# A fused mLSTM cell and SwiGLU block: the value halves of four weight pieces are asked for by GpSimd instead of ScalarE and SP

## The chip, the cores and the metric

The kernel runs on one core of one Trainium2 chip. The time is that of the device for one execution, in microseconds (us); three runs of the kernel before gave 554.77, 555.38 and 555.61, median 555.38. A profile shows one further execution.

The core has five engines, each with its own instruction stream in fixed order: TensorE (PE; its weight loads are listed as PEld), VectorE (DVE), ScalarE (ACT), GpSimd (POOL) and SyncE (SP, which here only asks for DMA transfers). ScalarE and GpSimd can ask for transfers too. All transfers run on 16 shared DMA engines; each asking engine has a queue of its own there. Engines and transfers wait for each other by semaphores.

## The reference

Two blocks follow each other. The first is an mLSTM cell over 4 batches, 8 heads, 768 steps and head size 40; the second a SwiGLU feed-forward layer on its output, 3072 tokens of 320 features, with 1536 hidden units.

```python
for t in range(S):                                   # per batch and head
    m_new = max(f[t] + m, i[t])
    C = exp(f[t] + m - m_new) * C + exp(i[t] - m_new) * outer(v[t], k[t])
    n = exp(f[t] + m - m_new) * n + exp(i[t] - m_new) * k[t]
    y[t] = sigmoid(o[t]) * (C @ q[t]) / max(abs(n @ q[t]), 1)
x = y, as (tokens, heads * head size)                # 3072 x 320
g = x @ w_gate;  val = x @ w_val                     # 320 x 1536 each
out = (g * sigmoid(g) * val) @ w_out                 # 1536 x 320
```

The three weights arrive as 64-bit floats; everything else is fp32.

## The kernel before, in words

**Stages.** The 768 steps are cut into six groups of 128 tokens for each of the 4 batches, so a group is 512 tokens wide for the feed-forward layer. For group g the kernel runs the 12 blocks of hidden units (`hidden(g, m)`, L643: 10 pairs of matmuls into two PSUM banks, one for gate and one for value, then SiLU on ScalarE, L653, and the product on VectorE, L654), with the mLSTM work of group g+1 set between the blocks by hand (`slots`, L727), and then the projection with `w_out` (L664, L671). The order of instructions on each engine is the order in which the program's text calls them.

**Start.** The first group's mLSTM part has functions of its own (`first_...`, L478 to L562). The calls from L564 to L611 are in the order that each engine follows. Among them are `sig(0)` and `sig(1)` (L463: sigmoid of o_sb on ScalarE, after its load), `first_gate(P)` (L541: two products on VectorE, then a small copy of x_sb on GpSimd, L545), `first_seam` (L555: transposes on PE and copies to xT by ScalarE and VectorE) and `first_state` (L547). `burn` (L466) keeps PE busy with matmuls whose result is not used.

**Weights.** A 64-bit weight is read as two 32-bit words and made into a 32-bit float on the chip. `PIECES` (L138) lists ten pieces: pieces 0 and 1 have one block of 128 hidden units each, pieces 2 to 6 two blocks each, always gate and value; pieces 7 to 9 are w_out. `piece_load(p)` (L140) asks for a piece. The gate half goes to partitions 0 to 63, the value half to partitions 64 to 127; a half of a two-block piece is 640 KB, 64 x 5 rows of 2 KB. The gate half is asked for by SP, the value half by ScalarE for pieces below 5 and by SP from 5 on (L146, L165). Pieces 0, 1, 4 and 5 land in the two buffers `raw` of a pool, piece 2 in a part of h_sb that is not in use yet and piece 3 in wo_sb.

A block j is then converted in three steps: `scale(j)` on ScalarE (L190 the high words, L192 the low words), `join(j)` on VectorE (L199, L200) and `rounded(j)` (L207) on GpSimd, except for block 0 and three later ones, where VectorE does it. Blocks 0 and 1 are converted before the first `hidden`; block m+2 is converted while `hidden(0, m)` runs for the first four (`ahead`, L725). ScalarE's part of block 2 stands in its stream before the SiLU of `hidden(0, 0)`.

**What stands around the change.** ScalarE asks for the value halves of pieces 2 and 3 right behind `sig(1)`, and for that of piece 4 behind `scale(0)`, before its copies for `first_seam(1)`. SP asks for the value half of piece 5 behind that piece's gate half; after it come the store of M_sb to M_dram (L611) and the loads of k and q for the second group (L117). GpSimd has, in this stretch, the two copies of `first_gate` and then `rounded(1)`, `rounded(2)` and so on; it asks for no transfer in the whole kernel.

Of the kernel before, what the change touches and what calls it, by code (L numbers as in the profile page):

```python
# [12 lines left out]
U32 = mybir.dt.uint32  # L13
# [11 lines left out]
def kernel(  # L25
# [18 lines left out]
    nc = tc.nc  # L44
# [12 lines left out]
    NKC = DM // HP  # L57
    UH = BH // 2
    UA = UH // 2
    NH = NFC + 1  # L60
# [15 lines left out]
    def bank(name, tag="cell"):  # L76
        return psum.tile([128, 512], F32, name=name, tag=tag)
# [23 lines left out]
    wo_sb = const.tile([128, NFC, DM], F32)  # L101
    h_sb = const.tile([128, NH, TW], F32)
# [34 lines left out]
    raws = {}  # L137
    PIECES = [("gv", 0, 1), ("gv", 1, 1)] + [("gv", m, 2) for m in range(2, NFC, 2)] + [("o", m, 4) for m in range(0, NFC, 4)]  # L138

    def piece_load(p, home=None):  # L140
        kind, m, n = PIECES[p]
        if kind == "gv":
            a, d = NKC, n * 128
            src = [(slice(i * HP, (i + 1) * HP), w[:, m * 128:(m + n) * 128].rearrange("(c p) f -> p c f", p=HP))
                   for i, w in enumerate((moe_w_gate, moe_w_val))]
            queues = (nc.sync, nc.scalar if p < 5 else nc.sync)  # L146
        else:
            a, d = n, DM
            src = [(slice(0, 128), moe_w_out[m * 128:(m + n) * 128].rearrange("(a p) d -> p a d", p=128))]
            queues = (nc.sync,)  # L150
        if src[0][1].dtype == F32:
            for r, w in src:
                if kind == "o":
                    nc.sync.dma_start(out=wo_sb[r, m:m + n, :], in_=w)
                else:
                    for x in range(n):
                        nc.sync.dma_start(out=wgv_sb[r, m + x], in_=w[:, :, ts(x, 128)])
            return
        if home is None:
            raw = conv.tile([128, 4 * NKC * 128], U32, name="raw")  # L160
        else:
            raw = home.rearrange("p a t -> p (a t)").bitcast(U32)
        raw = raw[:, 0:2 * a * d]
        for (r, w), queue in zip(src, queues):
            queue.dma_start(out=raw[r].rearrange("p (a d) -> p a d", a=a), in_=w.bitcast(U32))  # L165
        words = raw.rearrange("p (a d two) -> p a d two", two=2, a=a)
        raws[p] = (words[:, :, :, 0], words[:, :, :, 1])
        split(p)
# [4 lines left out]
    def split(p):  # L173
        if p in raws:
            lo, hi = raws.pop(p)
            kind, m, n = PIECES[p]
            if kind == "gv":
                for c in range(n):
                    r = slice(c * 128, (c + 1) * 128)
                    blocks[m + c] = (lo[:, :, r], hi[:, :, r], wgv_sb[:, m + c])  # L180
            else:
                for c in range(0, n, 2):
                    blocks[NFC + (m + c) // 2] = (lo[:, c:c + 2], hi[:, c:c + 2], wo_sb[:, m + c:m + c + 2, :])

    def scale(j):
        if j in blocks:
            lo, hi, dst = blocks[j]
            a, d = hi.shape[1], hi.shape[2]
            top = conv.tile([128, NKC * 128], F32, name="top", bufs=1).rearrange("p (a d) -> p a d", a=a)
            nc.scalar.mul(top, hi.bitcast(F32), 2.0 ** -112)  # L190
            low = conv.tile([128, NKC * 128], I32, name="low").rearrange("p (a d) -> p a d", a=a)
            nc.scalar.mul(low, lo, 2.0 ** -29)  # L192
            blocks[j] = (low, top.bitcast(U32), dst)
# [53 lines left out]
    for u in range(B):  # L247
        r = slice(u * BH, (u + 1) * BH)
# [213 lines left out]
    def sig(P):  # L462
        nc.scalar.activation(o_sb[:, heads(P)], o_sb[:, heads(P)], AF.Sigmoid)  # L463


    def burn(n, tag="cell"):  # L466
        t = bank("burn", tag)
        for _ in range(n):
            nc.tensor.matmul(t, lhsT=junk[:, 0:128], rhs=junk, start=True, stop=True)
# [57 lines left out]
    def first_own(u):  # L527
        first_y[u] = bank("first_y", "gen")[:, 0:H * D1].rearrange("p (h d) -> p h d", d=D1)
        for h in range(H):
            nc.tensor.matmul(first_y[u][:, h, :], lhsT=W0[:, u * H + h, :], rhs=v_sb[:, u * H + h, :], start=True, stop=True)  # L530

    def first_x(u):
        y = first_y.pop(u)
        den = work.tile([128, UH, 1], F32, name="den")[:, 0:H]
        nc.vector.tensor_scalar(den, y[:, :, D:], scalar1=1.0, scalar2=None, op0=ALU.max)
        nc.vector.scalar_tensor_tensor(den, in0=y[:, :, D:], scalar=-1.0, in1=den, op0=ALU.mult, op1=ALU.max)
        nc.vector.reciprocal(den, den)
        nc.vector.tensor_tensor(x_sb[:, u, 0:DM].rearrange("p (h d) -> p h d", d=D), y[:, :, 0:D],
                                den.to_broadcast([128, H, D]), op=ALU.mult)

    def first_gate(P):  # L541
        for u in (2 * P, 2 * P + 1):
            x = x_sb[:, u, 0:DM].rearrange("p (h d) -> p h d", d=D)
            nc.vector.tensor_tensor(x, x, o_sb[:, u * H:(u + 1) * H], op=ALU.mult)
        nc.gpsimd.tensor_copy(x_sb[:, 2 * P:2 * P + 2, DM:], x_sb[:, 2 * P:2 * P + 2, 0:HP])  # L545
# [33 lines left out]
    first_turn(1, q_sb, qT, (A, V))  # L579
    load(o_sb, o_gate, 0, 1)  # L580
    piece_load(0)
    piece_load(1)
    late_maxima()
    first_own(1)
# [2 lines left out]
    first_x(1)  # L587
    sig(0)
    sig(1)
    piece_load(2, h_sb[:, NH - NKC:])  # L590
    piece_load(3, wo_sb)
    burn(3)
    first_own(2)
    first_own(3)
    first_gate(0)
    first_x(2)
    first_x(3)
    first_seam(0, (A, A, V))
    scale(0)
    first_gate(1)  # L600
    burn(6, "gen")
    piece_load(4)
    join(0)
# [242 lines left out]
```

## Time and profile before

| | us |
|---|---|
| median of three runs | 555.38 |
| the profiled execution | 555.16 |
| its span, first to last instruction | 553.0 |
| PE busy (99% of the span) | 546.4 |
| VectorE busy (42%) | 234.4 |
| ScalarE busy (24%) | 134.7 |
| GpSimd busy (19%) | 106.6 |

The granted TensorE clock is at full speed throughout. 45.69 MB move in 223,994 packets; the DMA engines are busy nine tenths of the time in the first 83 us and less later. SP's queue (q1) carries 42.11 MB, ScalarE's (q10) 2.85 MB.

In a row of the timeline stand the start and the duration in us, the engine, the line of the program, the operation, output<-input with its size, and how often; in brackets how long the engine stood idle before it and what ended that. SPq, ACTq and POOLq are the instruction sequencers, where requests for transfers appear: their duration is that of asking, not of the transfer. The chain that ended last is followed back from the last instruction, at each step to what released it. Busy matmuls are modelled at their ends, so neighbouring rows overlap by some hundredths.

### The profile page before, as it was taken

The page shows a single profiled execution, that of the slowest core. Times are in us where ns is not written, and L with a number is a line of the kernel's source. Part 1 is how long each engine was busy: PE and PEld are TensorE (multiplying, and loading weights), DVE is VectorE, ACT ScalarE, POOL GpSimd, SP SyncE. Part 2 cuts the span into 40 slices and gives each one's busy share as a digit, 9 for nine tenths or more (in the row PEclk, how much of TensorE's full clock was granted, in tenths as well). Part 3 has the DMA queues.
Part 4 walks back from the last instruction along what each step waited for, and adds up shares of the span by engine and source line. Part 5 has one row for each costly group of instructions (what it writes and reads, how often), then busy time and mean ns, then how long its engine had stood idle before and what let it go on. Part 6 is the DMA issues. An engine that isn't in the chain of part 4 may idle for free.

```text
span 553.0 us, 11595 instructions
## 1 busy us (share of the span) xinstructions
PE 546.4 (99%) x4992; PEld 312.9 (57%) x4992; DVE 234.4 (42%) x394; ACT 134.7 (24%) x202; POOL 106.6 (19%) x97
## 2 busy tenths in 40 slices
PE   8999999999999999999999999999999999999997
PEld 4955546675545575544576455466455567444475
DVE  5956687962156332445521445531426621011100
ACT  4366564443101033110124101005110100111100
POOL 2314355574011151011133001114001200000000
PEclk9999999999999999999999999999999999999999
DMA  9999996798631763660464451395000131000000
GB/s 125 177 280 187 192 274 115 155 111 125 68 49 17 108 109 83 71 76 5 82 127 104 53 68 27 49 149 107 13 1 2 29 62 43 12 1 0 2 24 24
DMA packets 223994, 45.69 MB, mean 83 GB/s; under 512 B 214504, under 2 KB 219112, under 8 KB 223944
## 3 DMA queue, kind: packets, MB, share of 16 engines
q1 hardware_dynamic: 222036, 42.11, 46.7%
q10 hardware_dynamic: 1908, 2.85, 2.0%
q8 instruction: 39, 0.64, 0.5%
q14 instruction: 11, 0.09, 0.1%
HBM read 35.68 MB, written 4.01 MB: 72 GB/s over the span
## 4 chain that ended last, share of the span: by engine, by line
PE 92%; DMA 4%; SPq 3%; POOL 0%; DVE 0%; ACT 0%; issue 0%; ACTq 0%; POOLq 0%
PE gv_ps L648 55%; PE o_ps L664 24%; PE o_ps L671 5%; SPq L117 3%; DMA h_sb<-in_moe_w_val_dram 2%; PE inter L377 2%; PE sp L331 2%; PE intra L382 2%; DMA o_sb<-in_o_gate_dram 2%; PE add L353 1%; PE tp_kq L296 0%; POOL wgv_sb L207 0%; PE tp_x L439 0%; DVE wgv_sb L200 0%; ACT top L190 0%
## 5 line engine op out<-in xcount | busy, mean ns | idle before, releaser
L648 PE MATMUL gv_ps<-xT,wgv_sb 64*128 64x512 f32 x1440 | 317.3, 593 | 1.6 <-POOL wgv_sb L207 1.1
L648 PEld LDWEIGHTS gv_ps<-xT,wgv_sb 64*128 64x128 f32 x1440 | 139.1, 187 | 159.4 <-issue 154.6
L654 DVE TENSOR_TENSOR h_sb<-sg,gv_ps 128x512 f32<-128x512 f32 x72 | 49.5, 687 | 214.5 <-ACT sg L653 214.4
L664 PE MATMUL o_ps<-wo_sb,h_sb 128*128 128x320 f32 x480 | 130.5, 433 | 0.0
L664 PEld LDWEIGHTS o_ps<-wo_sb,h_sb 128*128 128x128 f32 x480 | 90.8, 190 | 41.0 <-issue 3.8
L653 ACT ACTIVATE sg<-gv_ps 128x512 f32<-128x512 f32 x72 | 43.0, 597 | 268.6 <-PE gv_ps L648 268.5
L362 POOL TENSOR_TENSOR C<-C,dec 128x328 f32<-128x328 f32 x20 | 14.5, 735 | 137.7 <-DVE C L369 137.6
L456 POOL TENSOR_SCALAR_AFFINE_SELECT w_sb<-w_sb 64x1024 f32<-64x1024 f32 x20 | 27.8, 1388 | 60.2 <-DVE w_sb L451 59.3
L658 ACT COPY z_sb<-o_ps 128x320 f32<-128x320 f32 x24 | 10.0, 422 | 94.7 <-PE o_ps L664 90.9
L403 POOL TENSOR_TENSOR o_sb<-o_sb,y_sb 128x640 f32<-128x640 f32 x10 | 14.3, 1428 | 79.2 <-DVE y_sb L394 79.1
L671 PE MATMUL o_ps<-wo_sb,h_sb 128*128 128x320 f32 x96 | 26.9, 437 | 0.0
L451 DVE TENSOR_TENSOR w_sb<-g_T,w_sb 128x1024 f32<-128x1024 f32 x10 | 13.2, 1355 | 27.6 <-DMA w_sb<-M_dram 27.6
L426 DVE STREAM_TRANSPOSE xT<-x_sq 128x640 f32<-128x640 f32 x16 | 12.5, 822 | 23.7 <-DMA x_sq<-x_sb 23.7
L671 PEld LDWEIGHTS o_ps<-wo_sb,h_sb 128*128 128x128 f32 x96 | 17.9, 190 | 7.2
L394 DVE TENSOR_TENSOR y_sb<-y_sb,intra 64x328 f32<-64x328 f32 x40 | 19.7, 493 | 0.8 <-PE intra L382 0.2
L369 DVE TENSOR_TENSOR C<-C,add 40x328 f32<-40x328 f32 (+1 forms) x36 | 17.7, 493 | 1.3 <-PE add L353 0.4
L207 POOL TENSOR_TENSOR wgv_sb<-wgv_sb,low 128x640 int32<-128x640 int32 x8 | 12.3, 1541 | 23.7 <-DVE wgv_sb L200 21.9
L377 PEld LDWEIGHTS inter<-C,qT 64*64 64x64 f32 x640 | 10.2, 134 | 7.3 <-issue 6.1
L341 POOL TENSOR_TENSOR vw_sb<-v_sb,w_sb 128x656 f32<-128x656 f32 x10 | 12.8, 1303 | 0.4
L338 DVE TENSOR_TENSOR w_sb<-sp,w_sb 128x512 f32<-128x512 f32 x20 | 12.7, 682 | 0.0
L460 ACT ACTIVATE w_sb<-w_sb 128x1024 f32<-128x1024 f32 x10 | 10.6, 1058 | 8.8 <-POOL w_sb L456 8.8
L397 DVE TENSOR_SCALAR den<-den 128x16 f32<-128x16 f32 x10 | 12.2, 1216 | 0.3
(129 smaller groups left out, 343.7 us busy)
## 6 DMA issues: line engine op xcount, KB each, us to landing
w_sb<-M_dram SPq DMA_DIRECT2D x10, 512.0 KB, 7.2
x_sq<-x_sb SPq DMA_DIRECT2D x128, 40.0 KB, 2.0
k_sb<-in_k_dram SPq DMA_DIRECT2D x12, 320.0 KB, 6.1
v_sb<-in_v_dram SPq DMA_DIRECT2D x12, 320.0 KB, 5.7
o_sb<-in_o_gate_dram SPq DMA_DIRECT2D x12, 320.0 KB, 5.4
raw<-in_moe_w_out_dram SPq DMA_DIRECT2D x3, 1280.0 KB, 7.8
out_dram<-z_sb SPq DMA_DIRECT2D x24, 160.0 KB, 1.8
q_sb<-in_q_dram SPq DMA_DIRECT2D x32, 64.0 KB, 2.4
```

The lines of the kernel that those rows point to most:

```text
L117: nc.sync.dma_start(out=dst[:, heads(P), 0:D], in_=tokens(a, c, P))
L362: nc.gpsimd.tensor_tensor(state(s + 1)[:, a], state(s)[:, a], dec[:, s - 2, a].unsqueeze(2).to_broadcast([128, UA, D1]), op=ALU.mult)
L369: nc.vector.tensor_tensor(c, c, ps[r], op=ALU.add)
L377: nc.tensor.matmul(inter[two][half(i), a, :], lhsT=qT[half(two), P * UA + a, half(i)], rhs=state(2 * n + i)[half(two), P * UA + a, :], sta ...
L394: nc.vector.tensor_tensor(t, t, intra[i][half(c)], op=ALU.add)
L403: eng.tensor_tensor(o, o, y[:, :, 0:D], op=ALU.mult)
L456: nc.gpsimd.affine_select(w, w, compare_op=ALU.is_ge, fill=NEG, base=0, pattern=[[0, UH], [1, SUB]], channel_multiplier=-1)
L648: nc.tensor.matmul(ps[i], lhsT=wgv_sb[half(i), m, PAIRS[kc][i] if g < 2 else kc, :], rhs=x[half(i), kc, :], start=(kc == 0), stop=(kc == N ...
L653: nc.scalar.activation(sg, ps[0], AF.Silu)
L654: nc.vector.tensor_tensor(hid(g, m), sg, ps[1], op=ALU.mult)
L664: nc.tensor.matmul(p, lhsT=hid(g, m)[:, ts(u, L)], rhs=wo_sb[:, m, :], start=(m == 0), stop=(m == NFC - 1))
L671: nc.tensor.matmul(ps[u], lhsT=hid(g, m)[:, ts(u, L)], rhs=wo_sb[:, m, :], start=(m == 0), stop=(m == NFC - 1))
```

## The change

Three things are different. The value halves of pieces 2 to 5 are asked for by GpSimd. For pieces 2 and 3 the two halves are asked for at different places in the text: the gate half where it was, the value half later, behind `first_gate(0)` and `first_gate(1)`, which end with a copy on GpSimd. And for this the requests of a piece are kept in a small list until they are made (`asks`, `value_half`). Pieces 4 and 5 are called where they were, so on GpSimd the request for piece 4 comes before `rounded(1)` and that for piece 5 between `rounded(1)` and `rounded(2)`. Sizes, buffers and the conversion are as before.

```diff
+    asks = {}
+
+    def value_half(p):
+        for ask in asks.pop(p, ()):
+            ask()
+
-    def piece_load(p, home=None):
+    def piece_load(p, home=None, later=False):
...
-            queues = (nc.sync, nc.scalar if p < 5 else nc.sync)
+            queues = (nc.sync, nc.scalar if p < 2 else nc.gpsimd if p < 6 else nc.sync)
...
-        for (r, w), queue in zip(src, queues):
-            queue.dma_start(out=raw[r].rearrange("p (a d) -> p a d", a=a), in_=w.bitcast(U32))
+        asks[p] = [lambda r=r, w=w, queue=queue: queue.dma_start(out=raw[r].rearrange("p (a d) -> p a d", a=a), in_=w.bitcast(U32))
+                   for (r, w), queue in zip(src, queues)]
+        asks[p].pop(0)()
+        if not later:
+            value_half(p)
...
-    piece_load(2, h_sb[:, NH - NKC:])
-    piece_load(3, wo_sb)
+    piece_load(2, h_sb[:, NH - NKC:], later=True)
+    piece_load(3, wo_sb, later=True)
     burn(3)
     first_own(2)
     first_own(3)
     first_gate(0)
+    value_half(2)
     first_x(2)
     first_x(3)
     first_seam(0, (A, A, V))
     scale(0)
     first_gate(1)
+    value_half(3)
     burn(6, "gen")
     piece_load(4)
```

## The prediction

> **What bounds the kernel now.** I read the page first. TensorE (PE) is busy for 99% of the span, and the chain that ended last is 92% PE; but two of its shares are not PE: 3% is SP's queue and 2% a value half on its way. Read in order of time, that chain shows where (columns: start us, duration us, what):
>
> ```profile
> 16.64 8.77 DMA o_sb<-in_o_gate_dram
> ...
> 25.42 0.01 ACT o_sb L463
> 25.43 13.59 DMA h_sb<-in_moe_w_val_dram
> ...
> 39.17 0.81 ACT top L190
> ...
> 40.01 0.51 DVE wgv_sb L199
> ...
> 40.54 0.84 DVE wgv_sb L200
> ...
> 41.51 1.54 POOL wgv_sb L207
> ...
> 43.10 4.80 PE gv_ps L648 x20
> ```
>
> The value half of piece 2 (the third) is asked for at 25.43, behind ScalarE's wait for o_sb, and lands at 39.02. Then ScalarE, VectorE and GpSimd convert block 2 in 4.08 us (39.02 to 43.10), and hidden(0, 2) starts. From 43.10 to the end the chain is PE, but for 0.33 us at 100.65 and the last copy. So a shift of hidden(0, 2) goes to the end one for one, as long as nothing behind it becomes late. How long PE stood is in its timeline:
>
> ```profile
> 31.90 4.56 PE L648 MATMUL gv_ps<-xT,wgv_sb 64*128 64x512 f32 x20 [0.53 <-DVE m_in L285]
> 36.39 1.13 PE L552 MATMUL add<-vw_sb,k_sb 128*64 128x41 f32 x32
> 37.45 4.56 PE L648 MATMUL gv_ps<-xT,wgv_sb 64*128 64x512 f32 x20
> 43.10 4.80 PE L648 MATMUL gv_ps<-xT,wgv_sb 64*128 64x512 f32 x20 [1.08 <-POOL wgv_sb L207]
> 47.83 0.49 PE L622 MATMUL tp_g<-ident,i_sb 32*128 32x32 f32 x5
> ...
> 53.52 8.85 PE L648 MATMUL gv_ps<-xT,wgv_sb 64*128 64x512 f32 x40
> ```
>
> PE has one hole, 1.08 us. Two blocks that follow each other without a hole take 8.85 us (last row; what follows them starts at 62.38, 8.86 after 53.52), so without it the transposes of L622 could start at 37.45 + 8.86 = 46.31 and not at 47.83: **1.52 us** is all that there is to win here (1.08 idle, 0.24 because the stalled block takes 4.80 and not 4.56, the rest overlap at the seam).
>
> Why 13.6 us for 640 KB? The queue totals of two windows, 26 to 32 us and 33 to 44 us (queue: packets, MB, share of 16 engines):
>
> ```profile
> q1 hardware_dynamic: 809, 1.17, 109.4%
> ...
> q10 hardware_dynamic: 953, 1.87, 53.4%
> q1 hardware_dynamic: 921, 1.79, 50.9%
> ```
>
> q1 is SP's queue, q10 ScalarE's (its 2.85 MB over the span are ScalarE's loads). From 26 to 32 us q10 moves nothing, though its request was out at 25.43 to 26.03; q1 alone brings 196 GB/s. From 33 us both run, 333 GB/s together, and q1 hardly suffers (0.195 MB/us before, 0.163 beside). In the window of 32 to 33 us q10 has its first 28 packets. So the value half stood some 6.5 us behind the gate halves of pieces 2 and 3, asked for by SP at 22.94 and 23.69, and then took 6.6 us (32.4 to 39.02).
>
> **What the Trainium skill says.** "Perfetto Trace Analysis", section "DMA Instruction — HWDGE (DVE, Sync)": the hardware descriptor generator is one block shared by two sequencers and locked until a DMA's descriptors are made. The silent q10 agrees. "DMA: Bandwidth & Descriptors", section "SWDGE vs HWDGE vs iDMA": a DMA of GpSimd has its descriptors made by software on GpSimd and put into rings of its own, and each DMA engine goes round robin over its queues; section "Latency and other measured facts": first byte after about 1 us, against 0.6. No DMA of GpSimd is in this trace. "SBUF — State Buffer", section "SBUF: two separate sides": a two-port VectorE operation and GpSimd lock each other out; a GpSimd DMA of 620 ns alone took 3100 ns beside a copy. The lock is visible here: L199 takes 0.49 us, but 0.89 at 49.39, beside GpSimd's L207 (48.37 to 49.92).
>
> **The change, part by part.**
>
> *Piece 2's value half.* It leaves ScalarE at 25.43 and stands on GpSimd behind first_gate(0)'s copy (25.88 + 0.29 = 26.17), 0.74 us later. Its cost on GpSimd, G, is not in the trace. Bounds: 0.6 (the hardware queues' issue rows, 0.59 to 0.63) and 3.1 (the skill's locked-out case); I take 1.3, near the unlocked end, as VectorE's operations between 26 and 28.6 are mostly PSUM readers or tiny. First packets at 26.17 + 1.3 = 27.5. With the 6.6 us that the same transfer took once it had begun, it lands at 34.1. ScalarE is free for scale(2) only at 35.52 (end of L609, 34.78 + 0.74), so scale(2) starts at 35.6, block 2 is ready 4.0 us later at 39.6, and PE wants it at 42.0. The hole is gone: **−1.52**.
>
> *What GpSimd must also do.* Queued behind the requests are the copy for first_gate(1) (29.09, VectorE releases it), rounded(1) (34.31) and rounded(2). From 26.17 until PE wants block 2 (41.85, one block pitch after 37.45) there are 15.68 us; the copy and two roundings take 0.29 + 1.53 + 1.53 = 3.35; so four requests may take 12.3, G ≤ 3.08 each. With 1.3: request 2 ends 27.5, copy 29.38, requests 3 and 4 end 32.0, rounded(1) runs at 34.31 as before, request 5 35.84 to 37.1, rounded(2) ends before 40. Cost nothing, hidden by GpSimd's idle time (2.92, 4.93 and 5.66 us before those three operations). A VectorE L199 locked out by a request (the ones at 32.8 and 36.5 could be) loses at most G; blocks 1 and 2 have 1.6 (35.84 to 37.45) and 2.3 us to spare.
>
> *Sharing with the gate halves.* hidden(0, 0) hangs without slack on piece 0's gate half: landed 28.42 (the row of L190 at 28.50 waited 0.39 for it), L190, L199, L200, L123, L207 on VectorE until 31.76, PE 31.90. If the new ring starts at 27.5, the last packets of that half meet competition; 0 to 0.5 us, I take **+0.1**, as it is nearly done. Piece 1's half (1.6 us spare) and piece 2's gate half (33.4, at 0.163 instead of 0.195 MB/us about 35) stay in front of their users: ScalarE takes piece 2 at 35.6.
>
> *ScalarE loses three issues* of about 0.6 us. Two stood in front of a wait for PE. The third (30.04 to 30.65) held two copies of xT until 30.69; they end 0.6 earlier, but VectorE's rounding of block 0 ends at 31.76 too, and PE starts after both: 0. Without that cover it would be worth up to 0.6.
>
> *SP loses one issue* and its 3.6 us wait (37.72), so M_dram and the loads of k and q for the next stage move some 4 us ahead. Their users come at 62 us and later: 0. Pieces 3 to 5 are asked for at 29.4, 30.7 and 35.8 (before: 26.07, 30.04, 37.72). On a ring of 0.17 MB/us they end near 36, 40 and 44; ScalarE takes them at about 43, 52 and 56 (before: 45.05, 53.65 and 58.61): 0.
>
> **Sum.** 555.16 (the profiled execution, span 553.0 plus 2.2 around it) − 1.52 + 0.1 = 553.74. The median, 555.38, lies 0.22 higher: **554.0 us**, −0.25%. Anything within 0.2% (1.1 us) is about what a measurement of this kernel can't tell from no change.
>
> **Rivals.**
>
> *The data comes no earlier (0.15).* If requests are served in the order asked whatever the ring, GpSimd's at 27 stands behind SP's at 23.69 as ScalarE's at 25.43 did, starts at 32.4, lands at 39.0: 555.4. For: q10's silence alone doesn't say whether generator or engines held it. Against: from 33 us on the engines take from both queues at once.
>
> *The hole is replaced (0.07).* A late gate half of piece 0 (0.5 us) or of piece 2, or wider tails, leave a gain of 0.2 to 1.0: 554.4 to 555.2. Against: both queues together move 333 GB/s, so the gate loses little.
>
> *GpSimd becomes the bound (0.20), the slower side.* Each request carries 320 rows of 2 KB. Past G = 3.08 GpSimd's own row of work from 26.17 to rounded(2) sets hidden(0, 2), late by 4G − 12.3. The gain is eaten at G = 3.5, and 0.2% is lost at 3.75. With G = 4: 555.38 − 1.52 + 3.7 = 557.6. For: the skill's locked-out 3.1 us, VectorE busy nine tenths of the time in 26 to 34 us, no DMA of GpSimd here to price. Against: most of those VectorE operations are not two-port ones (L199, 0.49 us, is), and the lock ends with each.
>
> **Numbers.** The forecast has 0.58, its own range 553.5 to 554.7 (landing of piece 0's half ±0.4, repeats ±0.3); below 554.27 lie 0.50 of it. The rest of it, the two rivals without gain and a little of the third give 0.30 within 0.2%; slower 0.20. The range 553.4 to 557.0 leaves out the larger values of G and little else.
>
> **What would show it.** Right: a new software queue with packets from about 27.5 us while q1 runs; scale(2)'s L190 at about 35.6 instead of 39.17, with no wait for the value half; no hole before the third block of L648, L622 at 46.3 to 46.4; L123's two ScalarE copies at 30.1; SP's M_dram near 34. Wrong: GpSimd's copy for first_gate(1) later than 29.1 or rounded(1) later than 34.4 (G too large), hidden(0, 0) later than 32.0 (piece 0's gate half), or the new queue silent until 32 us.

## The result, and the profile after

The changed kernel takes 556.44 us (median of 16 executions, 555.56 to 559.57); the kernel before, on the same chip in turn with it, 554.78 us (16 executions, 554.16 to 558.07). The ratio is 1.0029, 95% interval 1.0018 to 1.0039: **slower by 0.3%**, where 0.25% faster was forecast. The profiled execution of the changed kernel took 555.86 us with a span of 554.1, the one of the kernel before 555.16 with 553.0. The changed kernel's own lines move: L648 is L659 now, L622 is L633, L451 is L460, L207 is L216, L190 is L199.

The chain that ended last, of the changed kernel (start us, duration us, what):

```profile
25.95 0.23 POOL x_sb L554
26.18 12.52 DMA h_sb<-in_moe_w_val_dram
...
38.86 0.80 ACT top L199
...
41.20 1.53 POOL wgv_sb L216
...
42.77 4.80 PE gv_ps L659 x20
```

The value half of piece 2 is asked for by GpSimd right behind first_gate(0)'s copy, as forecast, and lands at 38.70 instead of 39.02. The other three steps of its conversion follow as before. So the hole of PE stays, a little smaller. In the timeline of the changed kernel:

```profile
42.77 4.80 PE L659 MATMUL gv_ps<-xT,wgv_sb 64*128 64x512 f32 x20 [0.72 <-POOL wgv_sb L216]
47.51 0.49 PE L633 MATMUL tp_g<-ident,i_sb 32*128 32x32 f32 x5
```

The transposes start at 47.51 and not at 46.3; 0.32 us is won of 1.52. Why the data came no earlier is in the queue totals of the same two windows as before the change, 26 to 32 us (first line) and 33 to 44 us (the others; queue: packets, MB, share of 16 engines):

```profile
q1 hardware_dynamic: 792, 1.18, 109.1%
...
q0 software_dynamic: 540, 2.02, 64.7%
q1 hardware_dynamic: 553, 1.07, 38.5%
```

GpSimd's queue, q0, moves nothing until its first packet at 33.30, 6.3 us after its request was out (26.18 + 0.84 = 27.02), just as ScalarE's q10 did. Then it takes more than its share: 2.02 MB in 11 us, against q1's 1.07. Before, q1 had 1.79 beside ScalarE's 1.87. The sum fell from 3.66 MB to 3.09.

What pays for that is what stands on SP's queue behind the gate halves. Of the timeline of the kernel before, SP's requests, VectorE's first use of w_sb and a stop of PE in `intra`:

```profile
39.01 11.05 SPq L117 DMA_DIRECT2D k_sb<-in_k_dram  x2
...
56.61 9.13 SPq L447 DMA_DIRECT2D w_sb<-M_dram  x2
...
70.97 1.22 DVE L451 TENSOR_TENSOR w_sb<-g_T,w_sb 128x1024 f32<-128x1024 f32 x1 [1.31 <-DMA w_sb<-M_dram]
...
100.98 0.67 PE L382 MATMUL intra<-v_sb,w_sb 64*64 64x41 f32 x30 [0.33 <-issue]
```

And of the changed kernel:

```profile
34.84 16.10 SPq L117 DMA_DIRECT2D k_sb<-in_k_dram  x2
...
57.93 9.00 SPq L456 DMA_DIRECT2D w_sb<-M_dram  x2
...
71.81 1.22 DVE L460 TENSOR_TENSOR w_sb<-g_T,w_sb 128x1024 f32<-128x1024 f32 x1 [2.47 <-DMA w_sb<-M_dram]
...
100.26 0.75 PE L391 MATMUL intra<-v_sb,w_sb 64*64 64x41 f32 x34
101.83 0.67 PE L391 MATMUL intra<-v_sb,w_sb 64*64 64x41 f32 x30 [0.81 <-issue]
```

SP asks for k_sb 4.2 us earlier, as the prediction said, but is not done asking until 50.94 (before 50.06): the request stands until the gate halves ahead of it are through. w_sb is asked for 1.32 us later and VectorE gets it 0.84 us later, after a wait of 2.47 us (1.31 before). And PE stops for 0.81 us in the middle of `intra` (0.33 us before).

**Where the time went.** The first matmul of the projection with `w_out` (into o_ps) is a good mark: everything before it is start and first group. It is at 96.59 before and at 96.96 after (+0.37: 0.32 won at 47 us, 0.69 lost between there and here). The stop in `intra` adds 0.48; the stretch from the mark to the last copy is 0.17 shorter otherwise; and from the last copy to the end of the span it takes 2.99 us and not 2.63 (+0.36). 0.37 + 0.48 − 0.17 + 0.36 = 1.04, which is the difference of the spans.

That is the sum for one pair of executions. Four further profiles, described below, are of kernels that up to 93 us are the kernel before (b_tail, b_p9late) or the changed one (a_again, a_p9late). The transposes start at 47.83, 47.80 and 46.45 in those of the kernel before and at 47.51, 46.71 and 47.64 in those of the changed kernel, so the 0.32 us won lie within the spread. VectorE's first use of w_sb is at 70.97, 71.13 and 70.20, against 71.81, 71.68 and 72.62, and the mark at 96.59, 96.56 and 95.34, against 96.96, 96.83 and 97.76: in both, the earliest of the changed kernel is behind the latest of the kernel before.

### The profile page after: what moved, and what is told of

The parts are those of the page before. It is cut to its first block, busy times and chain, and to the rows that moved or that the text cites. A ratio compares the mean times of both kernels' runs of the same rounds, so it can differ in the third digit from the quotient of the medians.

```text
span 554.1 us, 11605 instructions
## 1 busy us (share of the span) xinstructions
PE 547.1 (99%) x4991; PEld 315.8 (57%) x4992; DVE 234.4 (42%) x394; ACT 135.1 (24%) x202; POOL 109.6 (20%) x101
## 3 DMA queue, kind: packets, MB, share of 16 engines
HBM read 35.68 MB, written 4.01 MB: 72 GB/s over the span
## 4 chain that ended last, share of the span: by engine, by line
PE 95%; DMA 2%; DVE 1%; issue 0%; ACT 0%; POOL 0%; ACTq 0%; POOLq 0%; DVEq 0%
PE gv_ps L659 55%; PE o_ps L675 23%; PE o_ps L682 5%; DMA h_sb<-in_moe_w_val_dram 2%; PE inter L386 2%; PE sp L340 2%; PE intra L391 2%; PE add L362 1%; PE tp_kq L518 1%; PE first_y L539 1%; DVE h_sb L532 1%; PE burn L478 1%; PE sp L528 0%; PE wps L489 0%; PE tp_kq L305 0%
## 5 line engine op out<-in xcount | busy, mean ns | idle before, releaser
L659 PE MATMUL gv_ps<-xT,wgv_sb 64*128 64x512 f32 x1440 | 318.0, 593 | 1.0 <-POOL wgv_sb L216 0.7
L659 PEld LDWEIGHTS gv_ps<-xT,wgv_sb 64*128 64x128 f32 x1440 | 142.3, 187 | 156.4 <-issue 151.4
L465 POOL TENSOR_SCALAR_AFFINE_SELECT w_sb<-w_sb 64x1024 f32<-64x1024 f32 x20 | 27.8, 1388 | 63.1 <-DVE w_sb L460 62.2
L460 DVE TENSOR_TENSOR w_sb<-g_T,w_sb 128x1024 f32<-128x1024 f32 x10 | 13.2, 1354 | 30.6 <-DMA w_sb<-M_dram 30.6
L216 POOL TENSOR_TENSOR wgv_sb<-wgv_sb,low 128x640 int32<-128x640 int32 x8 | 12.3, 1540 | 21.2 <-DVE wgv_sb L209 19.4
L391 PE MATMUL intra<-v_sb,w_sb 64*64 64x41 f32 x640 | 11.6, 227 | 0.8 <-issue 0.8
```

Source lines behind the costliest of these rows:

```text
L391: nc.tensor.matmul(intra[i][half(c), a, :], lhsT=w_sb[half(i), h, :], rhs=v_sb[half(i), h, :], start=True, stop=True)
L465: nc.gpsimd.affine_select(w, w, compare_op=ALU.is_ge, fill=NEG, base=0, pattern=[[0, UH], [1, SUB]], channel_multiplier=-1)
L659: nc.tensor.matmul(ps[i], lhsT=wgv_sb[half(i), m, PAIRS[kc][i] if g < 2 else kc, :], rhs=x[half(i), kc, :], start=(kc == 0), stop=(kc == N ...
```

## The experiments

Three questions stood: what held GpSimd's first packets back, why later data came later, and what a start without the hole is worth. The kernels before and after were the measure on each chip; medians of the kernel before lay between 554.78 and 555.01.

### Why the new queue was silent

**m1_rings** runs transfers alone: gate halves of 640 KB on SP's queue and one value half from another engine, in several orders: in `phase` SP asks for the gate halves, then `asker` for the value half. The whole computation is left out.

```diff
+    def phase(gates, asker, delay):
+        for n in range(gates):
+            half_of(moe_w_gate, 2 * n, 0, nc.sync, g[n])
...
+            half_of(moe_w_val, 2, 1, asker, g[3])
```

> Left out: the whole computation; only transfers of 640 KB weight halves remain, in seven phases that wait for each other: GpSimd asks alone (first use), GpSimd alone again, ScalarE alone, three gate halves by SP with ScalarE asking for a value half some 2 us later, the same with GpSimd asking, one gate half with GpSimd, one with ScalarE. Theory 'backlog' (what SP has asked for earlier holds every later request, whatever its ring): alone, GpSimd's first packet comes 1 to 2 us after the request, in both of the first phases; beside three gate halves it comes only when some two of them have passed, 5 to 7 us after the request, for ScalarE and for GpSimd alike. Theory 'first use' (GpSimd's first request needs some 6 to 7 us to get going): the first phase has its first packet 6 us or more after the request, every later GpSimd phase 1 to 2 us, also beside three gate halves. Theory 'generator' (only hardware-made requests hold each other, my prediction): ScalarE's beside three gate halves late, GpSimd's 1 to 2 us.

GpSimd's first request of the kernel, at 20.49 us, had its first packets at 22.6, beside the last of three halves that SP had asked for at the start; the second, with nothing else under way, 1.4 us after it was asked for, as two requests of ScalarE did (1.5 and 1.4). Asked for right behind three gate halves it waited. Row of GpSimd in the timeline, and the queue totals of 50.2 to 56.6 us:

```profile
50.20 0.67 POOL L77 DMA_DIRECT2D g<-in_moe_w_val_dram  x1
```

```profile
q1 hardware_dynamic: 703, 1.37, 99.7%
q0 software_dynamic: 5, 0.02, 1.6%
```

So neither the first use of the ring nor GpSimd's making of the request holds it; what was already asked for by SP does. The theory 'generator', on which the prediction stood, expected 1 to 2 us here, and the first packets came 6.1 us after the request (5.4 us after it was out). The phase in which ScalarE was to ask behind three halves shows nothing: SP asked for these at 12 to 18 us, and they were through long before ScalarE's request at 41.82.

**m2_backlog** asks whether all of it goes first or only a part. It is m1 with no, one, two or four gate halves ahead, and with four loads of 160-byte rows ahead (the last argument); the computation is left out again.

```diff
-    phase(3, nc.gpsimd, True)
...
+    phase(0, nc.gpsimd)
+    phase(1, nc.gpsimd)
+    phase(2, nc.gpsimd)
+    phase(4, nc.gpsimd)
+    phase(4, nc.scalar)
+    phase(0, nc.gpsimd, 4)
+    phase(0, nc.scalar, 4)
```

> Left out: the whole computation; only transfers remain. In each phase SP asks for 0, 1, 2 or 4 gate halves of 640 KB (rows of 2 KB), and GpSimd, or in one phase ScalarE, for one value half some 2 us later; two phases have four loads of k (rows of 160 B) in front instead. Theory 'intake' (the DMA engines take in about 1 MB, 64 KB each, ahead of what they move, and a later request of any ring comes behind it): the first packet of the value half comes about 2 us after the request with 0 halves ahead, about 3 with 1, 5 to 6 with 2, and still 6, not 12, with 4; the same for ScalarE's request behind 4; under 3 us behind the small rows if the intake is counted in rows (32 to 64 per engine), 6 us if it is counted in bytes. Theory 'order' (requests are served in full in the order asked): with 4 halves ahead 11 to 12 us. Theory 'generator': GpSimd 2 us in every phase.

Behind four halves (2.6 MB) GpSimd's request of 47.38 had its first packets at 53.9, long before those halves were through. Queue totals of 47.4 to 53.8, 53.8 to 55, 61 to 67.8 and 67.8 to 69 us; ScalarE asked the same way at 61.30:

```profile
q1 hardware_dynamic: 701, 1.37, 107.1%
...
q0 software_dynamic: 47, 0.19, 64.5%
q1 hardware_dynamic: 51, 0.10, 41.3%
...
q1 hardware_dynamic: 742, 1.45, 106.7%
...
q1 hardware_dynamic: 79, 0.16, 53.1%
q10 hardware_dynamic: 73, 0.15, 48.1%
```

From the end of the request to the first packet it is 5.4 us behind three halves (m1, GpSimd) and 5.9 us behind four, from GpSimd and from ScalarE alike, and 1.24 and 1.26 MB of SP's packets start in between. With nothing ahead it is 0.7 to 0.8 us, behind loads with 160-byte rows 1.4 us from either (1,388 and 1,686 of these rows pass, 0.22 and 0.27 MB). So behind a long line of 2 KB rows a later request, hardware or software, comes after a bounded amount of them, some 1.2 MB, and not after all; from then on the queues share. Behind two halves the first packets came at 42.39, when those were nearly through. Behind one half the runs don't agree: in m2 it was nearly through when GpSimd asked; in m1, where GpSimd asked 0.2 us after SP, only 0.34 MB of it went first. The expectation 'intake' came true for four halves and for the small rows; with one and two halves the packets came earlier than it said.

The second thing to see is who gets what from then on. Beside ScalarE, q1 keeps half (79 packets of 2 KB against 73). Beside GpSimd it keeps a third: q0's packets are 4 KB (0.19 MB in 47), and the packets of the two queues are nearly equal in number (47 and 51).

### What a start without the hole is worth

**a_early** has the value halves of pieces 2 and 3 asked for where their gate halves are, so GpSimd asks some 2.8 us earlier.

```diff
-    piece_load(2, h_sb[:, NH - NKC:], later=True)
-    piece_load(3, wo_sb, later=True)
+    piece_load(2, h_sb[:, NH - NKC:])
+    piece_load(3, wo_sb)
```

> The changed kernel with the value halves of pieces 2 and 3 asked for by GpSimd where their gate halves are asked for (behind its product of L510, at about 22.5 us instead of 26.18 and 29.61). Theory 'backlog': the software queue's first packets still come at about 32 to 33.3 us, the landing of piece 2 stays at 38 to 39 us, the hole before the third block at 0.7 us; time as the changed kernel's. Theory 'first use': first packets 7.1 us after the request, at 29.6, landing at about 35, no hole. Theory 'generator': first packets at 24, landing before 32. With either of the last two the time goes down at most by what VectorE's wait for w_sb (L460) leaves: if that theory holds, PE's gain of 0.7 us at 43 is lost again by 82 us and the time is that of the changed kernel within 0.5 us.

Asked for at 23.37, first packet at 30.32 (6.1 us behind the request's end), landed at 36.15: there is no hole ahead of the third block, though PE starts the first block at 32.74, 0.8 us later than in the changed kernel, and the transposes start at 47.08. The expectation 'backlog' had the first packets at 32 us and the hole still there; only its wait of 6 us came true. The time is 556.04, ratio 1.0020 (1.0010 to 1.0030): still slower than before, and within 0.5 us of the changed kernel, as expected if w_sb sets the pace. Timeline of a_early, VectorE:

```profile
71.62 1.22 DVE L460 TENSOR_TENSOR w_sb<-g_T,w_sb 128x1024 f32<-128x1024 f32 x1 [2.71 <-DMA w_sb<-M_dram]
```

VectorE waits for w_sb until nearly the same moment as in the changed kernel (71.81), and the mark is at 96.76.

**b_first** tries to take the hole away without the software ring: the kernel before, with both halves of pieces 2 and 3 asked for ahead of the two sigmoids.

```diff
-    sig(0)
-    sig(1)
     piece_load(2, h_sb[:, NH - NKC:])
     piece_load(3, wo_sb)
+    sig(0)
+    sig(1)
```

> The kernel before with the gate and value halves of pieces 2 and 3 asked for ahead of the two sigmoids, so that ScalarE's requests don't wait for o_sb; no software ring. Both theories expect ScalarE's requests at about 23 to 24 us, right beside SP's, the value half of piece 2 landed by 36 us and no hole ahead of the third block (L622 at about 46.4). Theory 'the hole is worth nothing' (after 43 us it is later data, w_sb and the instructions of PE, that set the pace): ratio 0.999 to 1.001. Rival 'one for one' (as the prediction had it, a block 1.5 us earlier is an end 1.5 us earlier): ratio 0.9965 to 0.998.

No hole is left ahead of the third block, but neither expectation of the time came true: 556.87, ratio 1.0034 (1.0021 to 1.0046). The value halves now stood ahead in the line of the engines. From 24 to 28 us q10 moved 0.78 MB and q1 0.02, so the gate half of piece 0 came late, and with it the first block. Timeline of b_first, ScalarE and PE:

```profile
31.16 0.79 ACT L190 ACTIVATE top<-raw 128x640 f32<-128x640 f32 x1 [0.39 <-DMA raw<-in_moe_w_gate_dram]
...
34.90 4.56 PE L648 MATMUL gv_ps<-xT,wgv_sb 64*128 64x512 f32 x20 [0.28 <-DVE m_in L285]
```

The first block starts at 34.90 instead of 31.90, the transposes at 49.24 instead of 47.83, the mark is at 97.99 instead of 96.59. That lateness did go on one for one: 1.41 us at the transposes, 1.40 at the mark, 1.36 in the span.

Both results, and those below, follow one rule. PE needs 48.76 us from the transposes (L622, L633) to the mark where nothing stops it (read from the kernel before); and from the start of VectorE's first operation on w_sb to the mark there are 25.14 us (read from a_early). The mark is the later of these two arms, within 0.01 us, in all twelve profiled executions (us; the larger sum in bold):

| kernel | transposes + 48.76 | w_sb + 25.14 | mark |
|---|---|---|---|
| before | **96.59** | 96.11 | 96.59 |
| after | 96.27 | **96.95** | 96.96 |
| after, again (a_again) | 95.47 | **96.82** | 96.83 |
| a_early | 95.84 | **96.76** | 96.76 |
| a_wfirst | **96.99** | 95.12 | 96.98 |
| b_tail | **96.56** | 96.27 | 96.56 |
| a_p9late | 96.40 | **97.76** | 97.76 |
| b_p9late | 95.21 | **95.34** | 95.34 |
| c_three | 97.67 | **100.31** | 100.32 |
| a_act | **96.78** | 94.92 | 96.78 |
| a_only2 | **97.41** | 97.06 | 97.40 |
| b_first | **98.00** | 97.29 | 97.99 |

In this execution of the kernel before the second arm is only 0.48 us behind the first. With w_sb where it was, that is all that an earlier third block could have given. But w_sb itself varies: b_p9late is the kernel before up to 93 us, its o_sb landed earlier by chance, so ScalarE asked at 24.28 instead of 25.43. It has no hole, its w_sb is at 70.20, and its mark is 1.25 us earlier, of the 1.38 that the transposes are.

### The stop in `intra`, and the order on SP's queue

**a_wfirst** puts the loads of w_sb ahead of piece 6 on SP's queue.

```diff
-        1: [run(piece_load, 6, h_sb[:, NH - NKC:]), run(decay_rows)],
-        2: [run(late_turns), run(weights_load, 1), run(load_all, v_sb, v, 1)],
+        1: [run(weights_load, 1), run(piece_load, 6, h_sb[:, NH - NKC:]), run(decay_rows)],
+        2: [run(late_turns), run(load_all, v_sb, v, 1)],
```

> The changed kernel with the two loads of w_sb from M_dram asked for by SP ahead of the two halves of piece 6 instead of behind them. Theory 'w_sb' (the loss between 68 and 82 us is VectorE's wait for w_sb, which lands 0.8 us later than in the kernel before): w_sb lands some 5 to 8 us earlier, VectorE's wait of 2.5 us at L460 is gone, PE has no hole at 77 us, and the scores (L340) start at 81.3 instead of 82.0, so 0.7 us faster than the changed kernel. Rival (the loss is noise of instruction fetch or of the matmuls): the stretch from 68.4 to 82.0 stays at 13.6 us.

VectorE no longer waits for w_sb (69.98, no idle time), but the first block of that execution was 1.9 us later (PE's granted clock was 0.85 and 0.50 in 26 to 28 and 28 to 30 us), so the mark stood at 96.98 on the first arm, and the stop in `intra` grew to 1.45 us. 556.57, ratio 1.0028 (1.0014 to 1.0041), where 0.7 us less than the changed kernel was expected: in the profile what the wait gave back was lost elsewhere. Of its 22 executions only 7 had the full clock on the mean, with a median of 555.82 (changed kernel 556.18, 11 such); so some of it may have been gained, but that is few.

The stop looks like a fetch of PE's instructions. It is always behind the 34th matmul of `intra`, and on q8, the instruction queue, one packet of 16 KB starts 2.4 to 2.6 us before PE goes on; it starts only as the last of the 1280 KB of piece 9, on SP's queue, go. Queue totals of the changed kernel, 98.2 to 99.4 us and 99.3 to 101 us:

```profile
q1 hardware_dynamic: 192, 0.49, 101.4%
...
q1 hardware_dynamic: 42, 0.07, 10.3%
q8 instruction: 1, 0.02, 3.6%
```

It starts at 99.48 and PE resumes at 101.83; in the kernel before at 98.34 and 100.98; in a_early at 99.22 and 101.69. The Trainium skill, "Runtime: NRT & Kernel Launch", section "Instruction fetch mechanics", says that engines fetch 16 KiB blocks by a DMA queue of their own and that the cost is mostly hidden. A block of that size is seen here; behind this bulk transfer it is not hidden, as PE stops for 0.33 to 1.45 us.

**a_p9late** and **b_p9late** ask for piece 9 later, behind the loads of w_sb of the next group, in the changed kernel and in the kernel before.

```diff
-        11: [run(do_attend, 1, 0), run(do_gather, 1, 0, False), run(piece_load, 9)],
+        11: [run(do_attend, 1, 0), run(do_gather, 1, 0, False)],
...
-        1: [run(do_gather, 1, 1), run(weights_load, 2), run(load_all, v_sb, v, 2)],
+        1: [run(do_gather, 1, 1), run(weights_load, 2), run(piece_load, 9), run(load_all, v_sb, v, 2)],
```

> The changed kernel with piece 9 (1280 KB of w_out) asked for by SP behind the w_sb loads of the next group instead of ahead of them, so some 8 us later. Theory 'fetch' (PE's unexplained stop of 0.81 us at 101.0 is an instruction fetch, a 16 KB packet of queue 8, that stands behind piece 9's packets): the fetch packet comes before 98 us or at least with no transfer ahead of it, the stop at 101 us is gone (under 0.1), and the time falls by about 0.8 us to 555.6. Rival (the stop is a missing record or comes from VectorE): the stop stays at 0.8 us and the time at 556.4.

> The kernel before with the same move of piece 9. Theory 'fetch': its stop of 0.33 us at 100.65 goes, time 0.3 us lower (554.5). Theory 'SP chain' (what PE does at 97 to 101 us is set by how late SP's queue is): the changed kernel's handicap against the kernel before shrinks from about 1.6 us to about 1.1 when both have the move, as the two stops differ by 0.48 us.

The stop at 101 is gone from both, and the packet on q8 starts 0.3 us behind the mark in both (98.07 and 95.64), so it did stand behind piece 9. But piece 9 now came too late for its own user. Timeline of a_p9late, PE:

```profile
115.23 1.37 PE L448 MATMUL tp_x<-ident,x_sb 64*128 64x64 f32 x20 [1.03 <-ACT xT L121]
```

With a second hole of 0.60 us at 134.8, and 1.59 and 0.91 in b_p9late, both are slower, where 555.6 and 554.5 were expected: 557.82, ratio 1.0058 (1.0046 to 1.0070), and 558.62, ratio 1.0067 (1.0048 to 1.0087). The new holes are larger in the second, so the two times don't show what is left of the changed kernel's handicap.

**c_three** joins a_early, the late piece 9 and piece 6's value half on GpSimd.

```diff
-            queues = (nc.sync, nc.scalar if p < 2 else nc.gpsimd if p < 6 else nc.sync)
+            queues = (nc.sync, nc.scalar if p < 2 else nc.gpsimd if p < 7 else nc.sync)
```

> The changed kernel with three edits: value halves of pieces 2 and 3 asked for where their gate halves are, that of piece 6 by GpSimd too, and piece 9 late as above. If PE's end is set by the hole before the third block, by VectorE's wait for w_sb and by the fetch behind piece 9, all three go: no hole (as in the run with early requests), w_sb 2 to 3 us earlier since SP's queue is 640 KB shorter, no stop at 101. Then PE is ahead of the kernel before by up to 1.5 us plus 0.33, less 0.4 us for the longer end: 553.2 to 554.3. If the loss has another cause, about 556.

559.24, ratio 1.0072 (1.0059 to 1.0085), the slowest, where 553.2 to 554.3 was expected. In its profile GpSimd asks at 22.10, 1.3 us earlier than in a_early and just ahead of SP's gate half of piece 1 (22.43). The value half lands at 31.17, and that gate half only at 35.82 (before 30.17): a hole of 2.47 us at 39.83. The line of the engines works both ways, as in b_first. What SP asks for later slips too, and VectorE's first operation on w_sb to 75.17.

### The fixed cost of one software request, and the ring

**b_tail** is the kernel before with one more thing: the load of v_sb for the last group, which nobody waits for, is asked for by GpSimd (in two requests).

```diff
-        nc.sync.dma_start(out=dst[:, heads(P), 0:D], in_=tokens(a, c, P))
+        (nc.gpsimd if dst is v_sb and c == 5 else nc.sync).dma_start(out=dst[:, heads(P), 0:D], in_=tokens(a, c, P))
```

> The kernel before with one late load, that of v_sb for the last group, asked for by GpSimd instead of SP, long before it is needed. Theory 'tail' (a kernel that uses the software ring waits for one more set of semaphores at its end: 0.36 us of the changed kernel's longer span lie behind the last copy): the time is 0.2 to 0.5 us above that of the kernel before, and the stretch from the end of the last copy to the end of the span is about 2.8 us instead of 2.6. Rival: no difference, and the longer end is chance.

555.67, ratio 1.0012 (1.0001 to 1.0024). From the last copy to the end of the span: 2.82 us against 2.63. The profile doesn't show what is done there. The medians differ by 0.79 us, so the longer end accounts for 0.19 of it; the interval begins at 0.06 us, and the rest isn't explained.

The last four ran side by side: the changed kernel again, the changed kernel with its four value halves asked for by ScalarE at the same places, and the change reduced to piece 2 (b_first, above, was the fourth). The first edit is that of a_act, the others are a_only2's.

```diff
-            queues = (nc.sync, nc.scalar if p < 2 else nc.gpsimd if p < 6 else nc.sync)
+            queues = (nc.sync, nc.scalar if p < 6 else nc.sync)
...
-            queues = (nc.sync, nc.scalar if p < 2 else nc.gpsimd if p < 6 else nc.sync)
+            queues = (nc.sync, nc.gpsimd if p == 2 else nc.scalar if p < 5 else nc.sync)
...
-    piece_load(3, wo_sb, later=True)
+    piece_load(3, wo_sb)
```

> The changed kernel once more, as the measure for the three runs beside it. Every theory expects what the first comparison gave: slower than the kernel before by 0.2 to 0.4%, VectorE waiting more than 2 us for w_sb at about 72 us, a stop of 0.5 to 1 us on PE at about 101 us.

> The changed kernel with one thing undone: the four value halves are asked for by ScalarE, at the same places in the text, and not by GpSimd. No software ring is left; the requests stay separate, and SP still loses the value half of piece 5. Theory 'ring' (the loss is the software ring's: its 4 KB packets take two thirds of the engines beside SP's 2 KB packets, and the program ends about 0.3 us later for having used it): both rings share evenly, gate half of piece 5 lands before 48 us and not at 51, w_sb is waited for under 1.6 us, and the time is that of the kernel before, ratio 0.999 to 1.001. Rival 'order' (the loss comes of what stands where: the value halves in other places, SP's M_dram and k_sb ahead of them): the ratio stays at 1.002 to 1.004, whatever the ring.

> Of the change only piece 2 is left: its value half is asked for by GpSimd behind first_gate(0); pieces 3, 4 by ScalarE and piece 5 by SP as in the kernel before. Theory 'each half costs' (what is lost is lost in sharing, half by half): one of four halves shares, w_sb is waited for about as long as before, 1.2 to 1.6 us, and what remains is the later end of a program with a software ring: ratio 1.000 to 1.0015. Rival 'the end alone' (using the software ring once costs all of it, at the end of the program): ratio 1.002 to 1.004, and the time between the last copy and the end of the span is at least 1 us longer than 2.63. First packet of the software ring at about 33 us under both.

| kernel | median us | ratio to before | 95% interval |
|---|---|---|---|
| a_again | 556.32 | 1.0027 | 1.0017 to 1.0036 |
| a_act | 554.78 | 0.9989 | 0.9980 to 0.9998 |
| a_only2 | 556.82 | 1.0036 | 1.0024 to 1.0049 |

a_act decides between the two theories: **with the same requests in the same places of the text, but on ScalarE's ring, the loss is gone** (1.54 us between the medians), and the kernel is a trace faster than the kernel before. Rival 'order' falls. The same places are not the same times: ScalarE asks at 24.44, 28.97, 30.81 and 37.85, GpSimd at 26.18, 29.61, 30.28 and 35.85. But in a_early GpSimd asks ahead of all four times of ScalarE (23.37, 24.20, 30.70 and 36.65), and the loss is still there; so it isn't the time of asking. Queue totals of 33 to 47 us, kernel before:

```profile
q1 hardware_dynamic: 1225, 2.36, 61.6%
q10 hardware_dynamic: 978, 1.91, 43.3%
```

The changed kernel:

```profile
q0 software_dynamic: 690, 2.61, 64.6%
q1 hardware_dynamic: 716, 1.40, 38.7%
```

a_act:

```profile
q10 hardware_dynamic: 1225, 2.38, 56.9%
q1 hardware_dynamic: 2145, 1.95, 51.5%
```

a_only2:

```profile
q1 hardware_dynamic: 1074, 2.10, 57.2%
q10 hardware_dynamic: 642, 1.25, 28.8%
q0 software_dynamic: 176, 0.66, 18.5%
```

The sums are 4.27, 4.01, 4.33 and 4.01 MB. The software ring not only takes two thirds of what there is, there is less of it: 0.26 MB less in these 14 us, which at the 0.305 MB/us of the kernel before is 0.85 us; VectorE's first operation on w_sb starts 0.84 us late. That the two agree is no proof: a_act moves only 0.06 MB more than the kernel before and has w_sb 1.19 us earlier, with SP's queue shorter by the value half of piece 5. In a_act the gate half of piece 5 lands at 45.98 (before 46.04, after 51.15), SP's second request for k_sb is out at 47.29, and VectorE doesn't wait:

```profile
69.78 1.22 DVE L460 TENSOR_TENSOR w_sb<-g_T,w_sb 128x1024 f32<-128x1024 f32 x1
```

PE's stop in `intra` is gone as well (the fetch starts at 97.39), and the end takes 2.64 us.

a_only2 missed both expectations. Its time is that of 'the end alone', but its end takes 2.76 us, 0.13 more than before, and not 1 more. One half alone on the software ring costs about as much as four. Queue totals of 34 to 38 us, while it runs, a_only2 (the first three) and the kernel before:

```profile
q0 software_dynamic: 132, 0.53, 53.9%
q1 hardware_dynamic: 141, 0.28, 24.8%
q10 hardware_dynamic: 137, 0.28, 24.4%
...
q10 hardware_dynamic: 355, 0.70, 56.6%
q1 hardware_dynamic: 309, 0.60, 48.5%
```

The engines move 1.09 MB in these 4 us, and 1.30 in the kernel before. Piece 2's own value half lands at 39.85, 0.83 us later than from ScalarE; the transposes are at 48.65, the mark 0.81 later, the stop in `intra` 0.25 longer, the end 0.13: 1.19 of the 1.22 us between the spans. This sum too is of one profile, and its first block starts at 33.34, at a lower clock, so the share of the late half in the 0.81 us is argued.

**Was the hole always there?** In the profiled execution of the kernel before it was; in that of b_tail, which is the same program up to the last group, it was not, since PE came later. Busy times of 26 to 30 us (PE, PEld, DVE, ACT, POOL with counts; then PE's granted clock, DMA share, GB/s), kernel before:

```profile
26.00:30.00 4.00, 3.98 (x30) 2.99 (x30) 3.49 (x12) 2.73 (x5) 0.46 (x2) 1.00 1.12 197
```

b_tail:

```profile
26.00:30.00 4.00, 4.00 (x21) 3.39 (x21) 2.75 (x12) 2.05 (x5) 0.29 (x1) 0.57 1.13 197
```

There the granted clock of PE is 0.57 for these four us, hidden(0, 0) starts at 33.38 instead of 31.90, finds block 2 ready, and the transposes start at 47.80 instead of 47.83. In 14 of 25 executions of the kernel before beside a_act the mean clock was below 0.9985; their median is 554.87, that of the other 11 is 555.28. In 52 others, beside a_early, the medians are 554.93 and 554.83 (26 each). So the lower clock costs this kernel next to nothing, as one would expect if the hole swallows a slower start; then in up to half of the executions there was no hole to take away. The lower mean is not always this late start (c_three has a mean of 0.997 and starts its first block at 31.73), but six of the twelve profiles have it between 26 and 32 us (a_wfirst, b_tail, a_p9late, a_act, a_only2, b_first), with granted clocks of 0.50 to 0.86 in windows of 2 us, and start their first block at 33.30 to 34.90, instead of 31.47 to 32.74 in the other six. Single profiles of these two kinds can't be compared in the first 50 us without that. In a_act, which has no hole in its profile, 8 executions with the lower clock have a median of 554.96 and 5 with the full one 554.22; that is few.

## Why the prediction was wrong

The forecast was 554.0 us, 1.4 less than before; the median was 1.66 us more than before. Two steps failed: GpSimd's ring was to start at 27.5 us beside SP's, and started at 33.30; and what SP's queue loses by the sharing was put at 0, and measured 1.17 us (0.69 + 0.48) in this pair of profiles. The observable of the first rival came true (the new queue silent past 32 us, here until 33.3), but its time, 555.4, did not; and the third rival had the right sign, but not by its mechanism.

- **Piece 2's value half**: the request on GpSimd at 26.18 was right (26.17). "First packets at 26.17 + 1.3 = 27.5" failed: 33.30. Some 1.2 MB of SP's packets went first, and the new ring didn't pass them. The trace of the kernel before had the same in q10's silence of six us; the prediction read this as the generator's, but GpSimd's requests were held as long as ScalarE's. The first rival came nearest to the mechanism. The transfer then took 5.4 us (6.6 forecast), so 0.32 us was won in this pair of profiles and not 1.52. The skill's round robin ("DMA: Bandwidth & Descriptors", section "Queues, rings and completion order": turns by packet between queues that have work) holds here from 33 us on (540 and 553 packets to 44 us), not from the request on.
- **"A shift of hidden(0, 2) goes to the end one for one"** had a condition, "as long as nothing behind it becomes late", and failed on it, as w_sb became 0.84 us late. Even with w_sb in its place it holds only until w_sb sets the pace, which in the profile before is 0.48 us on, and that could have been seen. VectorE's 1.31 us wait for w_sb at 70.97 stood in that trace. a_early, with the hole gone and w_sb late, shows it; b_p9late, with w_sb early, kept 1.25 of 1.38 us to the mark.
- **What GpSimd must also do**: right. G is 0.67 to 0.84 us (1.3 taken, 0.6 to 3.1 as bounds), so the upper bound, the locked-out case, was not seen (that the 0.89 us of one L199 are such a lock isn't tested); first_gate(1)'s copy at 29.17 and rounded(1) at 34.37 are in time. The rival "GpSimd becomes the bound" is out.
- **Sharing with the gate halves**: wrong in size and in place. "Both queues together move 333 GB/s, so the gate loses little" took the pair SP and ScalarE as the measure for SP and GpSimd. Measured: 0.286 MB/us together from 33 to 47 us (0.305 before), and q1 at 0.100 instead of 0.169. The gate half of piece 0, on which +0.1 was put, was not touched (hidden(0, 0) at 31.94, before 31.90).
- **SP loses one issue**: "Pieces 3 to 5 … end near 36, 40 and 44 … 0" and "users at 62 us and later: 0" are the terms that cost the sign in this pair of profiles. The gate halves landed at 40.39, 46.76 and 51.15; no engine waited for them, but SP's queue did, and w_sb with it: 0.69 us between 47 us and the mark, then 0.48 at the stop in `intra`. That later users need more than a late first request, namely an empty queue ahead, was left out.
- **ScalarE loses three issues**: 0, as forecast.
- **The end of the program**: not in the sum. 0.36 us for four requests, 0.13 for one and 0.19 for two.

The terms with their measured sizes (−0.32, +0.69, +0.48, −0.17, +0.36) give the +1.04 us of the spans. The medians differ by 1.66, and the second profile of the changed kernel is 1.34 longer than that of the kernel before (stop in `intra` 1.14 us), so how the rest divides between the late w_sb and the fetch stays open. That the loss goes with the software ring is shown by a_act and a_only2: four halves on ScalarE's ring lose nothing, and one half on GpSimd's loses 1.81 us. How the ring's lower sum becomes that time is argued from single profiles.

## What to carry to other kernels

Before moving a request to another ring because its transfer starts late, look at what has been asked for ahead of it: here a new ring came behind the same 1.2 MB as the old one, and only an earlier request brought the data earlier, at the cost of what it then passed. Price a transfer on GpSimd's ring by what it takes from the other queues, and follow the slowed queue to its last user before writing zero beside it. And where a hole is to be filled, look for the next wait on each other engine: the smallest of those slacks is the most that can be won, and look at it in more than one execution: here the hole, of 1.08 us in one profile, was absent in two others.

## What the hardware showed that was not expected

- Six us of silence for a newcomer, ScalarE or GpSimd, behind a long line of 2 KB rows (5.4 to 6.4 us from the end of the request, while 1.22 to 1.26 MB pass, in m1, m2, before and after), 1.4 us behind 160-byte rows (0.22 to 0.27 MB): the amount that goes first is not a fixed number of bytes; a number of rows fits better. What holds the newcomer wasn't found.
- The software ring's packets of 4 KB against the hardware rings' 2 KB: 2.02 MB against 1.07 in 11 us side by side, and a lower sum (1.09 MB in 4 us with one software and two hardware queues, 1.10 with one of each, 1.30 with two hardware queues). Whether the packet's size or the ring lowers the sum wasn't separated.
- What looks like a 16 KB instruction fetch behind a 1280 KB transfer stops PE for 0.33 to 1.45 us; with the fetch 1 us earlier (a_act), the transfer out of the way (a_p9late, b_p9late) or PE itself later (b_first) it doesn't.
- The program ends 0.13 to 0.36 us later for having used GpSimd's ring.
